# Another table of queue places for the planned order of a conformer block's forward and backward pass

## The chip, the cores and the metric

The program runs on one core of a Trainium2 chip. A core has five engines that run side by side, each with an instruction queue of its own that is taken in order: PE (matrix products and transposes), DVE (vector operations), ACT (activation functions, casts and scaled copies), POOL (general vector work) and SP, which here only starts transfers. PEld in a profile is PE loading its stationary operand. Engines wait for each other by semaphores. The metric is the device time of one execution in microseconds (us).

## The reference

x and grad_out are (2, 4000, 144) in bf16; the kernel returns the output y, the gradient of x and the gradients of seven weights.

```python
xa = layernorm(x)
q, k, v = split(xa @ w_qkv, 3)
p = softmax(q @ k.T * D ** -0.5)               # 4000 x 4000 for each batch
glob = (p @ v) @ w_att_out
u, g = split(gelu(xa @ w_mlp_in), 2)
gc = depthwise_conv(layernorm(g), dw_csgu)     # 5 taps along time
loc = (u * gc) @ w_mlp_out
m = concat(glob, loc)
y = x + (m + depthwise_conv(m, dw_merge)) @ w_merge
# and the gradients of x and of all weights for grad_out
```

## The kernel before

Time is cut into tiles of 125 rows, 32 for each batch. One tile is one step of the attention, forward and backward in one pass. The scores of 125 rows against 4000 columns are made in four chunks of 1000 columns (`ps`, L1580 and L1587). DVE takes the row minimum of the negated scores of each chunk while it copies them to `Pbuf` (L1602) and joins the four (`nm`, L1604); ACT makes the exponentials (L1608). The second set of products in `ps`, the gradient of the probabilities, is cast by ACT to `Sbuf` (L1618) and multiplied with the probabilities by DVE (L1620). Transposing transfers on SP's queue turn `Pbuf` into `PT` (L1612) and `Sbuf` into `ST` (L1794). PE then makes the products with the transposed tiles, `yz` from `PT` (L1629) and `yz` from `ST` (L1667), and the products `X` of both untransposed tiles (L1714), which are added up in `acc` by ACT (L1718) and DVE (L1720). `qt` is the transposed query side of a later tile (L1572), `zt` what is made of `yz`'s result (L1679).

The local branch (gelu, its layer norm, the convolution and their gradients, lines 534 to 710, names that begin with `l_`) is cut into units that run beside the attention steps. Before the attention there is an opening (the class that loads and folds the weights, L119 to L300): ACT and SP start the loads of the raw weights into `raw` (L148, L149, L152); PE transposes some of them (L165, L166); ACT copies them to `two` (L167, L168), which begins with the load of its function table; products of the folded weights follow (L199), then columns and scaled weights (`cols` L212, `sWm` L233). Beside it x is loaded and normalised: DVE's statistics (L358), the normalised rows `xa_aug` (ACT L379, DVE L381, POOL L383), PE's transposes of them (`pt`, L388 and L392), and their copies (ACT L389, DVE L393). `warm` (L187) are matmuls without a use, which keep PE busy in the opening. Near the middle the second batch is prepared in the same way (loads L42, L43; statistics L451 to L458). After the last step, the merge loads `go_h` and `Yg` in blocks of 252 KB (L42, L43), adds up `Hps` on PE (L2000), makes y (L2098 to L2101) and the gradient of x (L2110 to L2127), and a last part makes the weight gradients.

The program is written in one order, and a planner then gives every queue its final order. The class `Planner` gathers the instructions into groups (one instruction each; for PE up to sixteen matmuls), numbers them in written order, and lays them out with a list scheduler over guessed durations. `LEAD` shifts the due time of kinds of groups. At the end of `plan` the table `MOVED` is applied: for each engine it names queue places and the group that shall stand there; all other groups keep their order and fill the places left.

```python
for e in E:
    m = self.MOVED[e]
    put = set(m.values())
    rest = iter([g for g in order[e] if g not in put])
    order[e] = [m[q] if q in m else next(rest) for q in range(len(order[e]))]
```

After that each instruction is tied to the one ahead of it on its engine, so that the queue holds exactly this order. A place in `MOVED` moves one group to it, and shifts all that stand between the old place and the new one by one.

Transfers started by SP and ACT use eight completion semaphores in turn, so an issue also waits until the transfer issued eight before it has landed.

Of the kernel before, what the change touches and what calls it, by code (L numbers as in the profile page):

```python
# [744 lines left out]
class Planner:  # L745
# [98 lines left out]
        "PE": {6: 10, 12: 15, 25: 19, 29: 21, 37: 25, 39: 26, 43: 27, 51: 334, 53: 342, 56: 28, 64: 33, 71: 37, 73: 38, 77: 329, 87: 42, 92: 43, 95: 44,  # L844
            99: 45, 104: 422, 106: 425, 113: 465, 114: 470, 122: 543, 141: 610, 143: 627, 145: 625, 159: 667, 160: 719, 170: 786, 173: 780, 181: 824,
            187: 820, 191: 870, 197: 873, 199: 923, 202: 930, 205: 958, 206: 959, 212: 972, 215: 973, 216: 1000, 220: 1022, 225: 1056, 227: 1075,
            232: 1096, 236: 1104, 246: 1169, 255: 1230, 256: 1222, 260: 1248, 283: 1362, 285: 1373, 288: 1396, 297: 1422, 298: 1431, 305: 1479, 307: 1492,
            308: 1473, 310: 1511, 324: 1570, 328: 1589, 339: 1663, 341: 1651, 342: 1652, 350: 1714, 352: 1723, 357: 1744, 360: 1765, 363: 1768, 382: 1879,
            383: 1910, 399: 1961, 406: 2011, 416: 2064, 419: 2067, 423: 2098, 437: 2149, 445: 2196, 451: 2210, 453: 2261, 455: 2263, 458: 2249, 463: 2311,
            474: 2356, 482: 2407, 492: 2449, 493: 2480, 495: 2467, 502: 2511, 503: 2508, 513: 2561, 516: 2574, 517: 2605, 522: 2606, 523: 2630, 530: 2647,  # L850
            531: 2649, 536: 2702, 540: 2708, 551: 2732, 553: 2787, 556: 2845, 561: 2828, 562: 2831, 564: 2921, 574: 2962, 577: 2957, 584: 2983, 587: 3028,
            605: 3064, 607: 3065, 621: 3173, 625: 3198, 629: 3188, 637: 3247, 638: 3248, 644: 3265, 645: 3283, 651: 3299, 658: 3327, 660: 3328, 675: 3386,
            677: 3387, 678: 3419, 684: 3427, 691: 3453, 694: 3489, 700: 3519, 705: 3552, 710: 3520, 715: 3557, 717: 3598, 719: 3622, 723: 3620, 739: 3696,
            744: 3741, 747: 3766, 757: 3798, 759: 3796, 762: 3818, 769: 3862, 779: 3904, 782: 3930, 786: 3949, 790: 3988, 813: 4084, 822: 4126, 824: 4127,
            826: 4145, 840: 4216, 842: 4235, 846: 4242, 851: 4278, 854: 4290, 858: 4317, 860: 4330, 869: 4368, 874: 4389, 883: 4425, 885: 4463, 888: 4464,
            894: 4498, 895: 4503, 899: 4518, 902: 4548, 911: 4570, 913: 4596, 915: 4607, 918: 4610, 920: 4638, 924: 4655, 940: 4718, 942: 4721, 944: 4749,
            953: 4780, 961: 4843, 963: 4850, 971: 4893, 974: 4915, 977: 4900, 978: 4925, 985: 4987, 990: 4990, 992: 4974, 1001: 5027, 1008: 5078,
            1019: 5134, 1028: 5178, 1032: 5174, 1034: 5195, 1037: 5230, 1041: 5218, 1046: 5274, 1050: 5311, 1054: 5312, 1067: 5362, 1075: 5408, 1086: 5448,
            1089: 5494, 1093: 5508, 1102: 5540, 1105: 5555, 1111: 5612, 1112: 5599, 1117: 5642, 1127: 5667, 1129: 5671, 1132: 5701, 1138: 5726, 1140: 5738,
            1148: 5786, 1156: 5811, 1161: 5881, 1163: 5882, 1175: 5947, 1176: 5919, 1180: 5982, 1182: 5992, 1203: 6075, 1206: 6076, 1208: 6119, 1214: 6128,  # L860
            1219: 6144, 1222: 6186, 1223: 6168, 1227: 6199, 1232: 6206, 1233: 6225, 1237: 6242, 1245: 6266, 1247: 6270, 1251: 6271, 1255: 6292, 1266: 6329,
            1268: 6331, 1273: 6318, 1281: 6335, 1282: 6393, 1283: 6394, 1287: 6402, 1288: 6403, 1289: 6418, 1291: 6419, 1301: 6491, 1302: 6500, 1305: 6516,
            1307: 6525, 1313: 6541, 1318: 6519, 1322: 6528, 1323: 6543, 1324: 6544, 1330: 6607, 1334: 6621, 1338: 6958, 1339: 6635, 1340: 6638, 1342: 6639,
            1346: 6960, 1353: 6671, 1358: 6961, 1360: 6714, 1361: 6715, 1364: 6723, 1365: 6680, 1373: 6850, 1376: 6900, 1380: 6832, 1384: 6875, 1390: 6920,
            1392: 6923, 1394: 6932, 1400: 6980, 1403: 6953, 1404: 6941, 1405: 6950, 1408: 6995, 1409: 6997, 1412: 7000, 1415: 6982, 1418: 7008, 1419: 6983,
            1420: 7056, 1421: 7011, 1424: 7009, 1425: 7012, 1429: 7071, 1430: 7049, 1434: 7108, 1435: 7110, 1438: 7148, 1440: 7151, 1442: 7043, 1443: 7115,
            1444: 7152, 1446: 7084, 1451: 7159, 1453: 7130, 1457: 7160, 1459: 7102, 1462: 7128, 1464: 7175},
        "DVE": {0: 68, 3: 8, 5: 94, 8: 95, 9: 93, 12: 109, 14: 99, 15: 106, 20: 105, 21: 104, 22: 101, 24: 102, 26: 114, 28: 149, 29: 147, 31: 148,
            33: 151, 34: 153, 37: 98, 43: 137, 44: 133, 48: 131, 49: 189, 50: 187, 51: 192, 53: 190, 54: 113, 56: 186, 58: 172, 61: 180, 63: 155, 64: 196,
            65: 195, 69: 174, 70: 213, 72: 219, 74: 194, 77: 217, 78: 235, 79: 233, 84: 268, 100: 396, 110: 419, 111: 466, 116: 490, 117: 491, 120: 492,  # L870
            122: 485, 123: 476, 126: 477, 127: 468, 128: 507, 130: 537, 132: 472, 133: 517, 141: 563, 146: 564, 149: 556, 150: 575, 155: 560, 158: 601,
            165: 618, 167: 636, 171: 640, 172: 695, 174: 648, 176: 641, 180: 661, 181: 697, 182: 664, 184: 698, 188: 686, 190: 744, 193: 743, 196: 709,
            199: 745, 202: 746, 203: 671, 204: 700, 207: 737, 208: 747, 209: 733, 211: 749, 215: 748, 219: 688, 220: 755, 222: 826, 223: 751, 224: 827,
            226: 742, 231: 793, 238: 794, 241: 828, 243: 829, 247: 811, 248: 889, 250: 825, 251: 836, 255: 821, 256: 831, 258: 890, 259: 839, 261: 901,
            264: 842, 265: 844, 266: 843, 269: 845, 270: 861, 271: 846, 272: 862, 275: 882, 276: 880, 279: 886, 280: 914, 283: 898, 286: 916, 287: 909,
            288: 924, 291: 994, 292: 993, 294: 910, 295: 933, 297: 911, 298: 918, 300: 912, 302: 995, 304: 996, 308: 997, 311: 1041, 313: 1042, 315: 1043,
            316: 998, 318: 982, 319: 1044, 323: 1023, 324: 1027, 334: 1046, 337: 1060, 338: 1050, 339: 1053, 341: 1047, 343: 1038, 346: 1055, 348: 1058,
            350: 1092, 356: 1085, 357: 1094, 358: 1135, 361: 1136, 362: 1095, 367: 1113, 371: 1124, 373: 1190, 375: 1142, 378: 1189, 379: 1139, 380: 1159,
            383: 1144, 384: 1170, 386: 1156, 387: 1161, 389: 1149, 391: 1178, 397: 1215, 401: 1180, 402: 1205, 403: 1198, 405: 1217, 408: 1231, 409: 1223,
            412: 1208, 413: 1211, 415: 1236, 416: 1249, 418: 1250, 433: 1343, 434: 1229, 435: 1344, 437: 1303, 438: 1345, 440: 1346, 446: 1348, 447: 1308,  # L880
            453: 1347, 455: 1326, 459: 1351, 463: 1363, 466: 1364, 467: 1393, 469: 1365, 470: 1394, 471: 1389, 477: 1395, 481: 1411, 483: 1400, 484: 1437,
            485: 1401, 486: 1417, 491: 1439, 493: 1440, 495: 1486, 498: 1460, 504: 1462, 506: 1497, 509: 1455, 510: 1448, 512: 1498, 515: 1441, 516: 1499,
            522: 1505, 524: 1482, 527: 1510, 530: 1534, 531: 1533, 533: 1514, 537: 1568, 545: 1552, 550: 1538, 552: 1508, 557: 1680, 558: 1605, 561: 1608,
            565: 1682, 570: 1631, 571: 1624, 577: 1688, 579: 1686, 580: 1628, 581: 1687, 582: 1636, 584: 1645, 585: 1641, 587: 1653, 589: 1650, 592: 1698,
            593: 1655, 595: 1701, 596: 1691, 597: 1699, 598: 1664, 602: 1675, 605: 1715, 606: 1700, 607: 1719, 609: 1724, 612: 1729, 614: 1726, 616: 1745,
            617: 1748, 618: 1734, 627: 1797, 629: 1781, 632: 1783, 634: 1834, 636: 1784, 638: 1810, 644: 1785, 649: 1814, 651: 1794, 654: 1837, 656: 1829,
            657: 1844, 661: 1917, 663: 1861, 665: 1847, 668: 1919, 670: 1920, 672: 1921, 673: 1825, 676: 1980, 678: 1981, 681: 1939, 683: 1912, 691: 1986,
            693: 1927, 694: 1989, 697: 1988, 703: 1999, 704: 1946, 705: 1948, 706: 1934, 707: 1953, 709: 1992, 710: 1962, 712: 1943, 717: 1977, 718: 1965,
# [1671 lines left out]
```

## Time and profile before

| | |
|---|---|
| median of 3 runs | 1230.99 us (1229.53 to 1231.92) |
| the profiled execution | 1230.49 us, its span 1228.7 us |
| mean granted clock of PE | 0.998 |
| PE, DVE, ACT, POOL busy | 1173.0, 1092.6, 937.3, 252.2 us |
| transfers | 196.28 MB, 160 GB/s in the mean |
| transposing transfers `PT`, `ST`, `qt`, `zt` | 126, 126, 62, 62 |

All times in the profile are counted from the start of the span. A row of a timeline has the start, the duration, the engine, the line and the operation, and in brackets how long the engine stood idle ahead of it and what ended that. A row of the chain of waits has a start, a duration and what the end of the program hung on in that time; for a transfer (DMA) it runs from its issue to its landing. A matmul's duration overlaps with that of the next one, since they are pipelined.

### The profile page before, as it was taken

How to read it: one execution, taken by the hardware profiler on the slowest of the kernel's cores; microseconds unless marked ns; L12 is line 12 of the kernel's file. 1: busy time of each engine (PE TensorE's matmuls, PEld its weight loads, DVE VectorE, ACT ScalarE, POOL GpSimd, SP SyncE). 2: the span in 40 equal slices, each digit the busy share in tenths (PEclk: the TensorE clock that was granted, in tenths of full speed). 3: DMA queues.
4: the chain of work that ended last, by engine and by line, in shares of the span. 5: the costliest groups of instructions: out<-in, count | busy, mean ns of one | idle time of the engine just before them, and what ended most of it. 6: DMA issues, size and time to landing. Idle time of an engine off the chain costs nothing.

```text
span 1228.7 us, 36356 instructions
## 1 busy us (share of the span) xinstructions
PE 1173.0 (95%) x14352; PEld 948.9 (77%) x14352; DVE 1092.6 (89%) x3204; ACT 937.3 (76%) x1705; POOL 252.2 (21%) x413
## 2 busy tenths in 40 slices
PE   6999999999999998999999999999999999999998
PEld 4677877777777776777777777778777777899997
DVE  7579999999999998987789999999999998869725
ACT  5899788788897966767988888898888866736541
POOL 7011212111021223210110211101121222124530
PEclk9999999999999999999999999999999999999999
DMA  4578888988697898978987788887888789977653
GB/s 133 130 131 172 162 153 156 166 165 174 130 176 147 157 180 168 197 135 188 177 168 149 145 179 155 162 149 159 166 156 162 151 152 200 177 195 189 168 131 82
DMA packets 672638, 196.28 MB, mean 160 GB/s; under 512 B 647411, under 2 KB 666885, under 8 KB 672445
## 3 DMA queue, kind: packets, MB, share of 16 engines
q1 hardware_dynamic: 671336, 192.56, 79.5%
q8 instruction: 112, 1.84, 0.6%
q0 software_dynamic: 592, 1.18, 0.3%
q14 instruction: 60, 0.49, 0.1%
q10 hardware_dynamic: 538, 0.21, 0.1%
HBM read 23.14 MB, written 16.69 MB: 32 GB/s over the span
## 4 chain that ended last, share of the span: by engine, by line
PE 47%; DVE 26%; DMA 12%; ACT 9%; issue 4%; SPq 1%; POOL 1%; ACTq 0%; DVEq 0%; POOLq 0%
PE X L1714 12%; PE ps L1580 9%; DVE Pbuf L1602 7%; PE yz L1667 6%; PE yz L1629 5%; PE ps L1587 4%; DMA PT<-Pbuf 4%; DVE acc L1720 4%; DVE Sbuf L1620 3%; DMA ST<-Sbuf 2%; ACT Pbuf L1608 2%; DVE l_prod L637 2%; PE po L2098 2%; DMA qt<-qb 2%; PE Hps L2000 2%
## 5 line engine op out<-in xcount | busy, mean ns | idle before, releaser
L1602 DVE TENSOR_SCALAR_CACHE_REDUCE Pbuf<-ps 125x1000 bf16<-125x1000 f32 x256 | 306.2, 1197 | 31.0 <-PE ps L1587 29.8
L1618 ACT CAST Sbuf<-ps 125x1000 bf16<-125x1000 f32 x252 | 251.9, 1000 | 84.1 <-PE ps L1587 81.6
L1608 ACT ACTIVATE Pbuf<-Pbuf,nm 125x1000 bf16<-125x1000 bf16 x256 | 285.5, 1139 | 29.7 <-DVE nm L1604 29.1
L1714 PE MATMUL X<-QBs,Sbuf 125*125 125x144 bf16 x2048 | 298.8, 229 | 2.5 <-DVE acc L1720 0.7
L1714 PE MATMUL X<-QBs,Pbuf 125*125 125x144 bf16 x2048 | 293.9, 226 | 0.4 <-POOL QBs L1651 0.3
L1714 PEld LDWEIGHTS <-Sbuf 125*125 125x125 bf16 x2048 | 260.3, 137 | 28.0 <-issue 26.9
L1580 PE MATMUL ps<-xaT_m,qt 128*125 128x500 bf16 x1024 | 262.7, 375 | 14.6 <-DVE Pbuf L1602 8.2
L1714 PEld LDWEIGHTS <-Pbuf 125*125 125x125 bf16 x2048 | 261.1, 137 | 4.3 <-issue 3.2
L1720 DVE TENSOR_TENSOR acc<-X,acc 125x432 f32<-125x432 f32 (+1 forms) x373 | 201.7, 550 | 11.6 <-PE X L1714 11.3
L1620 DVE TENSOR_TENSOR Sbuf<-Sbuf,Pbuf 125x1024 bf16<-125x1024 bf16 x252 | 172.2, 688 | 1.0 <-ACT Pbuf L1608 0.6
L1580 PEld LDWEIGHTS <-qt 128*125 128x125 bf16 x1024 | 123.9, 137 | 59.9 <-issue 14.6
L1667 PE MATMUL yz<-xa_aug,ST 125*125 125x144 bf16 x2048 | 150.9, 229 | 8.8 <-DMA ST<-Sbuf 6.3
L1629 PE MATMUL yz<-xa_aug,PT 125*125 125x145 bf16 x2048 | 149.4, 228 | 7.4 <-DMA PT<-Pbuf 6.9
L1667 PEld LDWEIGHTS <-ST 125*125 125x125 bf16 x2048 | 139.9, 138 | 17.0 <-issue 8.5
L1629 PEld LDWEIGHTS <-PT 125*125 125x125 bf16 x2048 | 137.5, 137 | 17.3 <-DMA PT<-Pbuf 9.8
L1587 PEld LDWEIGHTS <-qt 16*125 16x125 bf16 x1024 | 36.2, 128 | 98.7 <-issue 98.7
L1651 POOL TENSOR_TENSOR QBs<-g,g 125x144 bf16<-125x144 f32 x64 | 32.8, 513 | 384.0 <-ACT g L1650 229.5
L1587 PE MATMUL ps<-XR,qt 16*125 16x500 bf16 x1016 | 110.9, 420 | 0.0
L593 POOL TENSOR_TENSOR rsr<-ve,mhalf 125x2 f32<-125x2 f32 x32 | 25.7, 803 | 202.9 <-DVE ve L592 152.7
L637 DVE TENSOR_TENSOR l_prod<-ring,Wc 125x720 bf16<-125x720 bf16 x128 | 66.7, 535 | 0.1
L665 POOL TENSOR_SCALAR l_w<-ring,nc,c 125x144 f32<-125x144 bf16 x60 | 30.5, 515 | 138.6 <-DVE nc L661 90.7
L682 POOL TENSOR_TENSOR A_dwc<-l_fl,A_dwc 128x512 f32<-128x512 f32 (+2 forms) x48 | 36.5, 760 | 78.2 <-ACT l_fl L681 77.3
(547 smaller groups left out, 2057.7 us busy)
## 6 DMA issues: line engine op xcount, KB each, us to landing
Yn_d<-yn SPq DMA_DIRECT2D x64, 35.2 KB
Zn_d<-zn SPq DMA_DIRECT2D x64, 35.2 KB
ug_d<-ugr SPq DMA_DIRECT2D x32, 70.3 KB
PT<-Pbuf SPq DMA_TRANSPOSE x126
ST<-Sbuf SPq DMA_TRANSPOSE x126
go_h<-in_grad_out_dram SPq DMA_DIRECT2D x8, 252.0 KB
Yg<-ug_d SPq DMA_DIRECT2D x8, 252.0 KB
Yg<-Yn_d SPq DMA_DIRECT2D x8, 252.0 KB
```

Source lines behind the costliest of these rows:

```text
L637: nc.vector.tensor_tensor(prod[:, bi].rearrange("p a b -> p (a b)"), ring[:, a, p + bi:p + bi + 5, :].rearrange("p a b -> p (a b)"), W.Wc[ ...
L682: nc.gpsimd.tensor_tensor(acc, fl[r0:r1, 0:n], acc, op=ALU.add)
L1580: mm = nc.tensor.matmul(pp[r // 2][:, r % 2, 0:CH], QT[i][:, 2 * h, 0:PB], bs(i)[0].xaT_m[:, c * CH:(c + 1) * CH], start=True, stop=False)
L1587: nc.tensor.matmul(pp[r // 2][:, r % 2, 0:CH], QT[i][rs, 2 * h + 1, 0:PB], xr, start=False, stop=True)
L1602: nc.vector.tensor_scalar(pv(Pbuf, i % NPB, c2), src, -1.0, 3.0e38, op0=ALU.mult, op1=ALU.min, accum_out=NM[i][:, c2:c2 + 1])
L1608: nc.scalar.activation(v, v, ACT.Exp, bias=NM[i][:, 4:5], scale=-1.0)
L1618: nc.scalar.copy(pv(Sbuf, i % NDB, c2), src)
L1620: nc.vector.tensor_tensor(sc, sc, pchunk(i % NPB, c2), op=ALU.mult)
L1629: nc.tensor.matmul(Y, PT[0:PB, j, 0:PB], S.xa_aug[:, j, 0:D + 1], start=(j == 0), stop=(j == NB - 1))
L1667: nc.tensor.matmul(Z, ST[0:PB, j, 0:PB], S.xa_aug[:, j, 0:D], start=(j == 0), stop=(j == NB - 1))
L1714: nc.tensor.matmul(X[:, jj, :], l, r, start=(n_ == 0), stop=(n_ == len(ops) - 1))
L1720: nc.vector.tensor_tensor(av, X[:, 0:nj, :], av, op=ALU.add)
```

## The change

Only the literal table `MOVED` is exchanged. `LEAD`, the scheduler, the guessed durations and all that builds the program stay, so both programs hold the same 14352 matmuls, 2662 vector operations, 1712 activations and copies, 413 POOL operations and 931 transfers on SP's queue; only the order on the five queues differs. The table is 22 lines longer, so what stood on line 1580 stands on 1602 afterwards, and so on.

| engine | entries before | entries after | the same in both | group moved in both, to another place or the same |
|---|---|---|---|---|
| PE | 302 | 330 | 87 | 177 |
| DVE | 1123 | 1272 | 95 | 762 |
| Activation | 576 | 629 | 76 | 325 |
| Pool | 139 | 164 | 24 | 86 |
| SP | 475 | 507 | 26 | 327 |

The first entries of each engine, and those of SP in the last attention steps and the merge (places 716 to 745):

```diff
     MOVED = {
-        "PE": {6: 10, 12: 15, 25: 19, 29: 21, 37: 25, 39: 26, 43: 27, 51: 334, 53: 342, 56: 28, 64: 33, 71: 37, 73: 38, 77: 329, 87: 42, 92: 43, 95: 44,
+        "PE": {11: 163, 16: 167, 24: 19, 26: 20, 29: 21, 31: 22, 35: 25, 37: 26, 44: 27, 51: 334, 53: 28, 54: 342, 55: 29, 61: 31, 64: 33, 71: 37, 79: 38,
...
-        "DVE": {0: 68, 3: 8, 5: 94, 8: 95, 9: 93, 12: 109, 14: 99, 15: 106, 20: 105, 21: 104, 22: 101, 24: 102, 26: 114, 28: 149, 29: 147, 31: 148,
+        "DVE": {0: 68, 1: 9, 5: 94, 6: 95, 11: 91, 12: 106, 14: 111, 16: 99, 17: 104, 18: 110, 19: 101, 21: 102, 23: 107, 24: 105, 25: 148, 26: 98,
...
-        "Activation": {0: 55, 4: 57, 5: 58, 6: 56, 8: 123, 12: 244, 14: 252, 15: 245, 17: 126, 18: 134, 19: 249, 20: 247, 24: 128, 26: 253, 28: 177,
+        "Activation": {2: 58, 7: 57, 11: 126, 12: 59, 13: 247, 16: 141, 20: 128, 21: 250, 23: 248, 24: 56, 26: 253, 28: 249, 31: 60, 35: 216, 37: 212,
...
-        "Pool": {0: 86, 1: 70, 2: 71, 6: 83, 7: 85, 8: 87, 9: 52, 12: 49, 13: 51, 14: 48, 18: 136, 27: 214, 30: 387, 32: 221, 33: 264, 36: 144, 37: 181,
+        "Pool": {0: 86, 1: 70, 2: 47, 3: 49, 4: 51, 5: 71, 7: 84, 8: 50, 10: 82, 11: 52, 12: 87, 15: 103, 17: 136, 18: 132, 20: 142, 27: 236, 28: 260,
...
-        "SP": {5: 62, 7: 64, 9: 7, 11: 67, 12: 73, 13: 77, 15: 88, 18: 76, 19: 63, 20: 391, 22: 256, 23: 261, 24: 165, 25: 259, 26: 257, 27: 166, 28: 65,
+        "SP": {4: 5, 5: 62, 7: 7, 8: 78, 11: 6, 12: 75, 15: 88, 17: 72, 19: 81, 20: 256, 21: 165, 22: 77, 23: 261, 24: 391, 27: 355, 28: 73, 29: 258,
...
-            709: 6259, 710: 6092, 712: 6191, 715: 6125, 717: 6146, 718: 6174, 719: 6277, 721: 6194, 722: 6058, 723: 6158, 724: 6192, 725: 6258, 726: 6246,
-            727: 6222, 728: 6132, 730: 6213, 731: 6195, 732: 6214, 733: 6257, 735: 6221, 738: 6159, 740: 6273, 741: 6236, 742: 6280, 745: 6157, 751: 6372,
+            716: 6196, 717: 6106, 718: 6065, 720: 6146, 721: 6127, 722: 6246, 724: 6193, 725: 6221, 726: 6222, 727: 6281, 729: 6277, 730: 6258, 731: 6194,
+            734: 6236, 735: 6255, 737: 6259, 738: 6058, 739: 6157, 741: 6257, 742: 6213, 743: 6132, 744: 6298, 745: 6256, 750: 6388, 751: 6385, 752: 6372,
```

What it does at the places that matter below, in the names of the kernel:

- In the opening ACT starts three transfers (the two of w_qkv and dw_merge) ahead of its table load; the four of w_mlp_out and w_att_out stand behind, between its copies and scaled weights. Two of the `sWm` (L233) stand behind the `xa_aug` (L379) they stood ahead of. DVE's first minimum (L1602) stands ahead of the copy of the third block of transposes (L393). Of the warm-up matmuls, five stand ahead of the first L392 and four behind it, where there were one and five.
- At the batch change SP starts the loads of x (`xa_aug`) ahead of those of grad_out (`gq`).
- In the step near 600 us the sixteen matmuls of L1667 of one half of a tile stand some 8 us of PE's work later, next to those of the other half, and the scores stand ahead of the products `X` that they followed.
- In the last attention step the loads `go_h` and `Yg` of 252 KB that stood ahead of the transposing transfer `ST` in SP's queue stand behind it, and so do the other large ones of that stretch. PE's first `Hps` (L2000) stand behind the last product `X` of one more tile part, some 8 us of PE's work later.
- In all steady steps, single vector operations, activations, transfers and matmul groups change places with their neighbours.

422 rows, old and new, of the table MOVED are left out of this document.

## The prediction

> **What bounds the kernel now.** I read the page's busy times and its chain first, then the busy time of each engine by stage, then the timelines at the places where an engine that bounds a stage stands idle.
>
> ```profile
> PE 1173.0 (95%) x14352; PEld 948.9 (77%) x14352; DVE 1092.6 (89%) x3204; ACT 937.3 (76%) x1705; POOL 252.2 (21%) x413
> PE 47%; DVE 26%; DMA 12%; ACT 9%; issue 4%; SPq 1%; POOL 1%; ACTq 0%; DVEq 0%; POOLq 0%
> ```
>
> The whole program leaves PE idle for 1228.7 - 1173.0 = 55.7 us, DVE for 136.1. The shares are means over unlike stages, so the table by stage decides (columns: stretch, its length, then busy time and count of PE, PEld, DVE, ACT, POOL, the granted clock, the DMA share, GB/s):
>
> ```profile
> 30.00:97.00 67.00, 63.69 (x675) 46.28 (x674) 45.31 (x108) 63.59 (x133) 8.30 (x14) 1.00 0.62 126
> 100.00:450.00 350.00, 338.56 (x4035) 268.68 (x4032) 344.76 (x1010) 291.79 (x522) 62.49 (x94) 1.00 0.86 162
> 520.00:600.00 80.00, 78.70 (x957) 62.60 (x955) 66.93 (x154) 61.69 (x108) 9.13 (x19) 1.00 0.83 166
> 600.00:640.00 40.00, 35.44 (x400) 28.11 (x399) 29.60 (x79) 36.66 (x71) 3.49 (x5) 0.96 0.92 175
> 640.00:1000.00 360.00, 352.07 (x4216) 279.82 (x4214) 353.37 (x1019) 299.94 (x534) 60.78 (x94) 1.00 0.83 158
> 1050.00:1224.00 174.00, 171.37 (x2571) 160.99 (x2570) 116.24 (x419) 84.23 (x164) 52.05 (x80) 1.00 0.68 160
> ```
>
> ACT is close to the bound from 30 to 97 us, DVE from 100 to 450 (5.2 us idle) and from 640 to 1000 (6.6 us idle), PE from 520 to 600 and from 1050 to the end (2.6 us idle in 174). An order of the same instructions can only take idle time from the engine that bounds its stage. So the places to look at are the opening, the seams near 478 and 601 us, and the few waits of PE in the last stage.
>
> **The change, part by part.** Only the table of places is changed: the same matmuls, vector operations, activations and transfers, in another order on every queue. Nothing is removed or added, so every term is a wait that goes, shrinks or appears. I laid the new order beside the old one and looked up, at each stall of the old trace, where the waiting instruction and what it waits for now stand. The sum is made against the profiled execution, 1230.49 us: its span of 1228.7 and 1.8 around it.
>
> *The opening.* ACT now issues three transfers ahead of its table load where it issued seven. The four that go behind are these (start, duration), with what follows them on ACT:
>
> ```profile
> 4.57 0.44 ACTq L148 DMA_DIRECT2D raw<-in_w_mlp_out_dram  x1
> 5.17 0.38 ACTq L149 DMA_DIRECT2D raw<-in_w_mlp_out_dram  x1
> 6.19 0.34 ACTq L149 DMA_DIRECT2D raw<-in_w_att_out_dram  x1
> 7.28 0.39 ACTq L148 DMA_DIRECT2D raw<-in_w_att_out_dram  x1
> 7.71 1.28 ACT L167 ACT_TABLE_LOAD   x1 [7.71 <-DMA raw<-in_w_att_out_dram]
> 9.00 0.46 ACT L167 COPY two<-hps 128x144 bf16<-128x144 bf16 x2
> 12.80 0.71 ACT L233 ACTIVATE sWm<-raw,cols 128x144 bf16<-128x144 bf16 x2
> ...
> 29.90 1.13 ACT L1608 ACTIVATE Pbuf<-Pbuf,nm 125x1000 bf16<-125x1000 bf16 x1
> ```
>
> and this is what PE does meanwhile (in brackets the idle time ahead of it and who ended it):
>
> ```profile
> 7.97 0.18 PE L166 MATMUL hps<-ident,raw 16*16 16x16 bf16 x1
> 9.51 0.84 PE L199 MATMUL hps<-two 128*128 128x144 bf16 x4 [1.37 <-ACT two L167]
> 13.96 1.02 PE L388 MATMUL pt<-ident,xa_aug 125*128 125x125 bf16 x8 [3.18 <-ACT xa_aug L379]
> 15.83 1.27 PE L187 MATMUL warm<-wz 128*128 128x256 bf16 x5
> ```
>
> Four fewer issues are 0.44 + 0.38 + 0.34 + 0.39 = 1.55 us, so the table load can end 1.5 us or more earlier, at 7.4, and the copies are then held by PE's transposes, the last of which ends at 8.15. L199 should start 0.7 to 1.1 us earlier. On ACT the pair of L233 at 12.80 (0.71) now stands behind the last xa_aug that PE's L388 waits for, and one issue (0.44) ahead of it: 0.3 more. L388 thus starts 1.0 to 1.4 earlier, I take 1.2. Against it: of the warm-up matmuls (five in 1.27 us, 0.25 each), nine now stand between L388 and the first projection, where there were six: three more, about +0.7. The four issues, 1.55 us, now lie among ACT's copies; what hides them is ACT's waiting ahead of 29.90. If that cover is gone, they cost up to 1.55, since ACT bounds what follows.
>
> ```profile
> 22.76 0.69 DVE L393 COPY R<-pt 16x1000 bf16<-16x1000 bf16 x1 [1.42 <-PE pt L392]
> 23.48 1.20 DVE L1602 TENSOR_SCALAR_CACHE_REDUCE Pbuf<-ps 125x1000 bf16<-125x1000 f32 x1
> 29.71 0.16 DVE L1604 TENSOR_REDUCE nm<-nm 125x1 f32<-125x4 f32 x1
> ```
>
> DVE waited 1.42 us for transposes although the scores of the first L1602 were ready; now L1602 stands ahead of that copy. It brings up to 1.42, and nothing where PE's later scores set nm (29.71); I take 0.5. The opening: -1.2 + 0.7 - 0.5 = -1.0, with the ends +0.7 (the warm-up alone counts) and -2.6 (all of 1.2 and 1.42).
>
> *The batch change.* The loads of x for the second batch move ahead of the loads of grad_out in SP's queue. The chain of waits and DVE's timeline show
>
> ```profile
> 478.27 5.17 DMA xa_aug<-in_x_dram
> 483.54 0.73 DVE L451 BATCH_NORM_STATS2 pst<-xa_aug 125x6 f32<-125x144 bf16 x3 [0.59 <-DMA xa_aug<-in_x_dram]
> ```
>
> The transfer is 5.17 us long, but DVE stood still for 0.59 of it only. Gain 0 to 0.6, I take 0.2.
>
> *The seam at 601 us.* Here everything stood still behind one transposing transfer:
>
> ```profile
> 596.22 5.41 DMA ST<-Sbuf
> 601.67 1.77 PE L1667 MATMUL yz<-xa_aug,ST 125*125 125x144 bf16 x16 [1.55 <-DMA ST<-Sbuf]
> 602.77 0.46 DVE L577 TENSOR_TENSOR l_z<-l_a,l_hs 125x576 bf16<-125x576 bf16 x1 [2.29 <-ACT l_a L574]
> 606.53 1.20 DVE L1602 TENSOR_SCALAR_CACHE_REDUCE Pbuf<-ps 125x1000 bf16<-125x1000 f32 x1 [2.06 <-PE ps L1587]
> 604.92 0.52 ACT L1718 COPY acc<-X 125x432 f32<-125x432 f32 x1 [0.21 <-PE X L1714]
> 607.43 0.52 ACT L1718 COPY acc<-X 125x432 f32<-125x432 f32 x1 [1.32 <-PE X L1714]
> ```
>
> PE waits 1.55 us in front of that L1667, with the products X and the next scores queued behind it; ACT and DVE then wait for those. In the new order these sixteen matmuls stand some 8 us later, next to their other half, and the scores ahead of the products. ACT carries this stage (36.66 of 40), so the gain is at most its two waits, 0.21 + 1.32 = 1.53. I take 1.0: what L1667 feeds comes later, and something of the wait can come back there. Ends 0 and -1.5.
>
> *The last attention step.* SP issues two loads of 252 KB each just ahead of a transposing transfer:
>
> ```profile
> 1066.52 0.34 SPq L42 DMA_DIRECT2D go_h<-in_grad_out_dram  x1
> 1069.37 0.58 SPq L42 DMA_DIRECT2D Yg<-ug_d  x1
> 1070.12 8.26 DMA ST<-Sbuf
> 1078.42 1.23 PE L1667 MATMUL yz<-xa_aug,ST 125*125 125x144 bf16 x16 [1.79 <-DMA ST<-Sbuf]
> 1070.00:1080.00 10.00, 8.21 (x119) 7.31 (x117) 5.91 (x11) 4.41 (x7) 1.64 (x3) 1.00 0.98 197
> ```
>
> It lands after 8.26 us, where the one above took 5.41, and PE, which bounds the stage, waits 1.79 us: all that PE lacks in these 10 us (8.21 busy). In the new order both loads, and the other large ones of this stretch, stand behind that transfer. 2.85 us less of landing would cover the 1.79. I take -1.5, since small loads still stand ahead; ends 0 and -1.8. What is late next are the loads themselves: they feed L2000, which the new order puts behind some 8 us more of PE's products, about as far as the loads move.
> The Trainium skill ("DMA: Bandwidth & Descriptors", section "Queues, rings and completion order") says that each transfer engine takes one issuer's descriptors in the order of the ring. By that alone the 504 KB ahead, at the 197 GB/s of the row, would be 2.6 us of the 8.26 (an estimate), this term -1.8 and the sum -4.0.
>
> *Everything else.* The steady stages have hundreds of entries of their own. Waits that the old trace shows there are often answered by a producer that stands 0.6 to 2 us earlier; what other instructions now wait for, the old trace cannot show. The gain cannot exceed DVE's idle 5.2 + 6.6 us; a loss is bounded by nothing but the waits that exist. I take 0, with 3 us to either side: a quarter of that idle time.
>
> The sum is -1.0 - 0.2 - 1.0 - 1.5 = -3.7: 1230.49 - 3.7 = 1226.8. The median of the three runs, 1230.99, lies 0.5 above the profiled one, so 1227.3; I say 1227.2.
>
> **The rivals.**
>
> *No change that can be measured, about 1230.* The gains lie at seams; the stages behind are bound by another engine. For it: of 67 us from 30 on, ACT is busy 63.59, and now has four issues (1.55) to place before it, so the opening can come to +0.7; DVE's late data at 601 can return as a wait for the moved L1667 (its 1.55). Then only the -1.5 at 1078 is left, with half a microsecond of losses: 1230.99 - 1.0 = 1230. Against it: the two PE and ACT waits are on the engine that bounds the stage.
>
> *Slower, about 1235: transposing transfers come late.* PE's waits for transfers were
>
> ```profile
> PE yz L1629 <- DMA PT<-Pbuf: 6.9, 12, 0.9
> PE yz L1667 <- DMA ST<-Sbuf: 6.3, 5, 1.8
> PE ps L1580 <- DMA qt<-qb: 4.8, 6, 1.2
> ```
>
> 18.0 us in 23 waits, 0.78 each, over 64 tiles. SP's queue is taken in order; its table changes most of its places, and every load or store that moves ahead of a transpose delays it, as at 1070. Against the sum of -3.7, 0.2% slower (2.5) needs 6.2 us, eight more such waits on the path. Ten give 7.8: 1227.3 + 7.8 = 1235. For it: DVE leaves so little idle that one late tile is not made up. Against it: the worst two of these waits, 1.79 and 1.55, are the ones that the order undoes.
> The Trainium skill's rule on the same page ("Rules for kernel authors") is to issue a transfer early and wait late; the loads that the change moves behind would by it be exposed in turn. No row here shows it yet.
>
> *Much faster, about 1222.* The ends add up: -2.6 - 0.6 - 1.5 - 1.8 = -6.5, and -3 from the steady stages: 1221.5. For it speak the many earlier producers; against it, that all ends must come together.
>
> **How the numbers follow.** The forecast has 0.48 (its own range 1224.5 to 1228.4), much faster 0.07, no change 0.19, slower 0.26. What a measurement of this kernel can tell from no change is about 0.2%, 2.5 us: faster 0.55, same 0.19, slower 0.26. The range goes from 1221.5, the sum of the ends, up to 1234.5, near the slower case, with about 0.07 left below and 0.12 above.
>
> **What would show it.** In the changed profile: the table load starting near 5 to 6 us and L388 near 12.8; the first exponential (29.90) near 29; no wait of DVE for x near 483; no wait over 1 us at L1667 near 600, and DVE not idle for over 2 us there; ST near 1070 landing in 6 us or less and PE over 9.5 busy in the ten microseconds after. DVE's idle time from 100 to 450 and 640 to 1000 should stay near 12 us, PE's waits for PT, ST and qt near 18 less 3.3. I am wrong if these waits grow by 6 us, or if DVE's idle time in the steady stages moves by more than 3.

## The result, and the profile after

| | before | after |
|---|---|---|
| median | 1231.45 us (1229.53 to 1232.70, 4 runs) | 1216.04 us (1212.67 to 1222.33, 4 runs) |
| the profiled execution | 1230.49 us, span 1228.7 | 1215.52 us, span 1213.7 |
| mean granted clock of PE | 0.998 | 0.999 |

The ratio is 0.9882, with an interval of 0.984 to 0.9925: 1.2% faster, 15.4 us by the medians. A second set of runs, told below, gave 0.9907 (0.9873 to 0.9941). The direction was predicted, the time was not: 1227.2 was said, and the range ended at 1221.5. Lines of the kernel after are 22 higher (1580 is 1602 now), those of the experiments' kernels 45 higher.

The busy times and the shares of the chain:

```profile
PE 1168.9 (96%) x14352; PEld 947.3 (78%) x14352; DVE 1085.6 (89%) x3204; ACT 936.3 (77%) x1705; POOL 254.7 (21%) x413
PE 55%; DVE 20%; ACT 12%; DMA 8%; issue 3%; SPq 2%; POOL 1%; ACTq 0%; DVEq 0%; POOLq 0%
```

The chain hangs on transfers for 8% of the span where it was 12%. DVE's idle time fell by 8.0 us (136.1 to 1213.7 - 1085.6 = 128.1), and its busy time by 7.0, though it runs the same instructions. The second number is the one that the prediction had ruled out.

The table by stage of the kernel after, in the columns of the prediction:

```profile
30.00:97.00 67.00, 63.35 (x678) 46.57 (x677) 46.67 (x114) 64.42 (x136) 8.88 (x17) 1.00 0.66 133
100.00:450.00 350.00, 342.80 (x4092) 272.08 (x4091) 348.16 (x1028) 293.94 (x528) 64.81 (x98) 1.00 0.85 166
520.00:600.00 80.00, 77.01 (x929) 61.24 (x929) 64.48 (x149) 67.56 (x120) 7.35 (x13) 1.00 0.87 175
600.00:640.00 40.00, 37.62 (x457) 30.25 (x455) 36.62 (x108) 34.96 (x65) 3.74 (x7) 1.00 0.81 163
640.00:1000.00 360.00, 353.82 (x4231) 281.77 (x4230) 353.17 (x1026) 298.67 (x532) 67.20 (x96) 1.00 0.82 161
```

A stretch of fixed times holds other work after an order has changed, so its idle time is compared with care. DVE's idle time from 100 to 450 went from 5.2 to 1.8 us and from 640 to 1000 from 6.6 to 6.8; ACT's from 30 to 97 went from 3.4 to 2.6.

The longest sums of PE's waits (in total, times, longest):

```profile
PE ps L1602 <- DVE Pbuf L1624: 7.2, 14, 0.9
...
PE yz L1651 <- DMA PT<-Pbuf: 3.9, 5, 1.9
...
PE ps L1602 <- DMA qt<-qb: 1.6, 1, 1.6
...
PE pm L1945 <- POOL Yr L2007: 1.4, 1, 1.4
...
PE yz L1689 <- DMA ST<-Sbuf: 0.9, 2, 0.4
```

Waits of PE for `PT`, `ST` and `qt` are 3.9 + 1.6 + 0.9 = 6.4 us in 8, where they were 18.0 in 23; the longest one for `ST` is now 0.4.

To see where the 15 us lie, the trace is cut where DVE joins the minima of a tile (`nm`), which every tile does once. This is worked out from the two traces, in us:

```
tiles            start  0-4   4-10  10-16  16-25  25-34  34-37  37-45  45-59  59-63   end
before            29.7  69.7  96.6   99.1  149.8  147.8   56.3  125.1  231.1   60.0  163.5
after             28.7  68.3  96.9   96.0  147.0  144.4   53.9  128.5  224.3   61.9  163.8
difference        -1.0  -1.4  +0.3   -3.1   -2.8   -3.4   -2.4   +3.4   -6.8   +1.9   +0.3
```

There is no one place: five stretches gain 2 to 7 us each, two lose 2 to 3. These are two single executions; what is chance in them shows only beside the traces of the experiments.

### The profile page after: what moved, and what is told of

Its sections match the earlier page's. It is cut to its first block, busy times and chain, and to the rows that moved or that the text cites. A ratio compares the mean times of both kernels' runs of the same rounds, so it can differ in the third digit from the quotient of the medians.

```text
span 1213.7 us, 36291 instructions
## 1 busy us (share of the span) xinstructions
PE 1168.9 (96%) x14352; PEld 947.3 (78%) x14352; DVE 1085.6 (89%) x3204; ACT 936.3 (77%) x1705; POOL 254.7 (21%) x413
## 4 chain that ended last, share of the span: by engine, by line
PE 55%; DVE 20%; ACT 12%; DMA 8%; issue 3%; SPq 2%; POOL 1%; ACTq 0%; DVEq 0%; POOLq 0%
PE X L1736 15%; PE ps L1602 10%; PE yz L1651 7%; PE yz L1689 7%; DVE Pbuf L1624 5%; PE ps L1609 4%; DVE acc L1742 3%; DMA PT<-Pbuf 3%; ACT Sbuf L1640 3%; DVE Sbuf L1642 3%; ACT Pbuf L1630 3%; PE po L2120 2%; PE Hps L2022 2%; DVE l_prod L637 1%; DMA ST<-Sbuf 1%
## 5 line engine op out<-in xcount | busy, mean ns | idle before, releaser
L1630 ACT ACTIVATE Pbuf<-Pbuf,nm 125x1000 bf16<-125x1000 bf16 x256 | 287.4, 1142 | 29.5 <-DVE nm L1626 28.8
L1602 PE MATMUL ps<-xaT_m,qt 128*125 128x500 bf16 x1024 | 261.2, 375 | 10.6 <-DVE Pbuf L1624 7.2
L1602 PEld LDWEIGHTS <-qt 128*125 128x125 bf16 x1024 | 123.6, 137 | 54.0 <-issue 12.2
L1673 POOL TENSOR_TENSOR QBs<-g,g 125x144 bf16<-125x144 f32 x64 | 33.9, 529 | 415.2 <-ACT g L1672 312.2
L665 POOL TENSOR_SCALAR l_w<-ring,nc,c 125x144 f32<-125x144 bf16 x60 | 32.7, 550 | 135.5 <-DVE nc L661 60.0
L2147 ACT ACTIVATE t<-t,dx_c,rstd_x 125x144 f32<-125x144 f32 x64 | 28.8, 500 | 32.5 <-DVE t L2146 32.4
```

Source lines behind the costliest of these rows:

```text
L1602: mm = nc.tensor.matmul(pp[r // 2][:, r % 2, 0:CH], QT[i][:, 2 * h, 0:PB], bs(i)[0].xaT_m[:, c * CH:(c + 1) * CH], start=True, stop=False)
L1630: nc.scalar.activation(v, v, ACT.Exp, bias=NM[i][:, 4:5], scale=-1.0)
L1673: nc.gpsimd.tensor_tensor(QBs[:, i % NPB, 1, :], g0[:], g1[:], op=ALU.add)
```

## The experiments

Each kernel has a table that names every place of every queue. `old[e]` and `new[e]` are the orders of queue `e` in the kernels before and after, `t[g]` is the start of group `g` in the trace of before. Cuts were put where both orders have done nearly the same work. Ratios are to the kernel before on the same chip, with a 95% interval; times are medians, and a gain in us is the ratio's distance from 1, of 1232 us.

### How far into the program the gain is made

```diff
-    order[e] = old[e]
+    order[e] = [g for g in new[e] if t[g] < END] + [g for g in old[e] if t[g] >= END]
```

with END at 99, 445, 640 and 1000 us.

> The changed order on all five queues for the work that started in the first 99 us of the old trace, the old order for everything after. Theory spread (the gain is made a little at a time in every stage, most of it in the steady ones, where I had put 0): 2 to 3 us faster than before, as the two traces differ at the fifth tile (99.37 against 96.98). Rival seams (the gain sits at a few places of the opening, the batch change, 601 and the last step, each worth more than I thought): 4 us or more faster here. Rival tail of the execution (the two traces differ by chance and the curve of progress cannot be read): anything else.

> The changed order up to 445 us of the old trace (the steady stage of the first batch with it), the old one after. Spread: 8 us faster than before (444.96 against 436.87 at the 26th tile), so 5 to 6 more than with the opening alone. Seams: no more than the opening alone gives, 2 to 4 us.

> The changed order up to 640 us of the old trace, the old one after. Spread: 13 to 14 us faster than before (649.07 against 635.16), the batch change and the stage of ACT up to 640 giving 5 to 6 of them. Seams: 4 to 6 us in all.

> The changed order up to 1000 us of the old trace, the old one in the last steps, the merge and the end. Spread: 16 to 17 us faster than before, which is 1 to 2 us faster than the whole change, since from the 60th tile to the end the changed trace lost 2. If the term of the last step was right after all, this kernel is 1 to 2 us slower than the whole change.

| changed up to | ratio | median, us |
|---|---|---|
| nothing | 1 | 1233.08 (18 runs) |
| 99 us | 0.9951 (0.9934 to 0.9968) | 1227.23 |
| 445 us | 0.9934 (0.9909 to 0.9960) | 1225.93 |
| 640 us | 0.9876 (0.9852 to 0.9901) | 1218.84 |
| 1000 us | 0.9873 (0.9845 to 0.9901) | 1218.42 |

Two stretches make most of the gain: the first 99 us (-6.0) and 445 to 640 (-7.1). The steady stages add 2.1 and 0.4, which the intervals do not tell from nothing.

### One queue's order at a time

```diff
-    order["SP"] = old["SP"]
+    order["SP"] = new["SP"]
```

The other queues are moved only as far as their dependences then force. `a_dve` does the same with DVE; `b_sp` is the kernel after with SP's queue back in the old order.

> The old order with SP's queue alone in the changed order; on the other queues only what SP's order forces is moved. Theory transfers (the changed order gains because transposing transfers reach PE in time: PE's waits for PT, ST and qt fell from 18.0 us to 5.5 + about 1): most of the gain, 8 us or more faster than before, with PE's waits for transfers under 10 us. Rival vector (DVE's own order makes the gain, by less idle time and fewer operations beside POOL's): under 3 us. Rival fit (only all queues together gain): no faster, or slower than before.

> The old order with DVE's queue alone in the changed order, the others moved only as far as that forces. Transfers: under 3 us faster than before, PE's waits for transfers still 15 us or more. Vector: 8 us or more faster. Fit: no faster, or slower than before.

> The changed order with SP's queue put back into the old order, the others moved only as far as that forces. Transfers: at 1225 us or above, within 5 us of before. Vector: within 4 us of the whole change. Fit: slower than the whole change by 8 us or more, and not faster than before.

They gave 1.1204 (1.1176 to 1.1232), 1.0864 (1.0837 to 1.0890) and 1.2218 (1.2187 to 1.2250): 1382, 1340 and 1507 us. PE's longest waits with SP's queue alone changed

```profile
PE yz L1674 <- DVE zn L1716: 24.7, 13, 5.5
```

and with SP's alone put back

```profile
PE ps L1625 <- DVE Pbuf L1647: 52.7, 47, 9.1
PE yz L1674 <- DVE zn L1716: 48.7, 21, 8.8
```

are for DVE, not for transfers. PE's clock suffers as well: in the three profiles it was granted at half for 120, 41 and 205 us, where the profile of before has 3.4. These kernels are not one queue's order alone, though. To fit SP's new order, 112 instruction groups of PE, 140 of DVE and 77 of ACT had to leave the old one, and those queues then follow neither kernel. So the runs show that an order so mixed loses 9 to 22%; how much of that comes from the one queue and how much from the forced moves is open, and so is whether any single queue "has" the gain.

### The middle alone, and its parts

```diff
-    order[e] = old[e]
+    order[e] = [g for g in old[e] if t[g] < A] + [g for g in new[e] if A <= t[g] < B] + [g for g in old[e] if t[g] >= B]
```

with A and B at 445 and 640; at 459.4 and 570.1 (the batch change); at 570.1 and 624.35 (the seam near 601).

> The changed order only for the work that started between 445 and 640 us of the old trace (batch change, the stage in which PE and then ACT bound), the old order before and after. The kernels with the changed order up to 445 and up to 640 differ by 7 us. If stages add up: 5 to 9 us faster than before. If the gain there hangs on where the stages before it end: under 3 us.

> The changed order only for the work that started between 459.4 and 570.1 us of the old trace, where both orders have done the same work at both ends: the batch change. Prediction: 0.2 us faster, at most 0.6. If stages add up (0.9924 for 445 to 640 less 0.9966 for 570 to 624): 4 to 6 us faster.

> The changed order on all queues only for the work that started between 570.1 and 624.35 us of the old trace, where both orders have done the same work at both ends; the old order elsewhere. Theory clock (a long wait of PE there costs its length and then 3.4 us at half the granted clock, in nearly every run): 4 to 6 us faster than before, the tiles 35 and 36 together 34 us long instead of 36 to 40. Rival, my own step (only the wait of 1.55 us is to be had, ACT's two waits bound it): 1 to 1.5 us faster.

445 to 640 alone gave 0.9924 (0.9902 to 0.9947), the batch change 0.9963 (0.9947 to 0.9978), the seam 0.9966 (0.9949 to 0.9983). In us that is -9, -4.6 and -4.2; the two parts add up to the whole.

At the seam the two stalls of PE are gone. Its rows with the seam alone changed

```profile
612.21 2.19 PE L1712 MATMUL yz<-xa_aug,ST 125*125 125x144 bf16 x32
615.54 2.24 PE L1674 MATMUL yz<-xa_aug,PT 125*125 125x145 bf16 x32
```

have no wait ahead of either. The trace of before has the 1.55 that the prediction showed and a second one behind it:

```profile
616.79 2.24 PE L1629 MATMUL yz<-xa_aug,PT 125*125 125x145 bf16 x32 [0.89 <-DMA PT<-Pbuf]
```

That profile was a mild one. The kernel with the first 99 us changed has the old order here, and shows

```profile
602.28 1.23 PE L1712 MATMUL yz<-xa_aug,ST 125*125 125x144 bf16 x16 [2.92 <-ACT l_a L574]
617.73 3.88 PE L1674 MATMUL yz<-xa_aug,PT 125*125 125x145 bf16 x32 [2.69 <-DMA PT<-Pbuf]
```

2.92 + 2.69 instead of 1.55 + 0.89 (the wait is put down to whichever came last, here ACT). In seven traces with the old order here the first of these stalls lasted 1.0 to 3.5 us. The second lasted 0.9 to 2.8 in five of them, in two put down to `qt`, and two have none. Over the same seven traces, the two tiles of this seam took 36.0 to 39.5 us, 37.8 in the mean, and the 36.0 is the one that was priced. Seven traces with the changed order gave 33.3 to 35.0, 33.9 in the mean. The difference, 3.9, agrees with the 4.2 measured.

At the batch change the wait that the prediction named has stayed, at 0.60 with this stretch alone changed:

```profile
477.83 0.73 DVE L451 BATCH_NORM_STATS2 pst<-xa_aug 125x6 f32<-125x144 bf16 x3 [0.60 <-DMA xa_aug<-in_x_dram]
...
468.52 0.64 DVE L670 SCALAR_TENSOR_TENSOR l_dd<-l_dgn,rsr,l_w 125x144 bf16<-125x144 bf16 x2
```

What went is something else, in the second row. In the trace of before the same operation of DVE stands beside POOL's sums:

```profile
466.85 1.27 POOL L682 TENSOR_TENSOR A_dwc<-l_fl,A_dwc 128x512 f32<-128x512 f32 x1
...
466.81 1.47 DVE L670 SCALAR_TENSOR_TENSOR l_dd<-l_dgn,rsr,l_w 125x144 bf16<-125x144 bf16 x1
...
469.32 0.63 DVE L670 SCALAR_TENSOR_TENSOR l_dd<-l_dgn,rsr,l_w 125x144 bf16<-125x144 bf16 x1
```

It takes 1.47 us instead of 0.36, and ends 0.16 after POOL does (466.81 + 1.47 against 466.85 + 1.27). With the changed order two of them take 0.64 together: 1.4 us of DVE's time are gone, and in all seven traces with the changed order here neither takes more than 0.37. That is 1.4 of the 4.6; where the other 3.2 come from the traces do not settle (tiles 25 to 34 are only 0.7 shorter in this kernel's profile than before's 147.8, and 1.3 shorter than the mean of the other traces with the old order here).

### Which queues the seam needs

```diff
-    order["PE"] = old["PE"]
+    order["PE"] = [g for g in old["PE"] if t[g] < 570.1] + [g for g in new["PE"] if 570.1 <= t[g] < 624.35] + [g for g in old["PE"] if t[g] >= 624.35]
```

for PE alone (30 places), for SP alone (45 places), and for both.

> As the last, but only PE's queue takes the changed order in that stretch (30 places; three on DVE move with it). If the later place of the sixteen matmuls and the earlier scores make the gain, as the prediction had it: as fast as the kernel with all queues changed there, within 2 us. If the order of the queues has to fit together even here: no faster than before, or slower.

> The old order, with only SP's queue in the changed order between 570.1 and 624.35 us of the old trace (45 places; five on PE and three on ACT move with it). Theory transfers (in the old order PT is issued behind the acc_d stores, the ring store and qt, and PE then waits 0.9 to 2.8 us for it near 617 in five of five traces; the changed order issues it earlier): 3 to 5 us faster than before, no wait of PE for PT over 1 us near 617, tile 36 at 14 to 15 us. Rival fit: SP's order alone gives nothing, as PE's alone did, under 1.5 us either way.

> The old order, with PE's and SP's queues in the changed order between 570.1 and 624.35 us of the old trace (30 and 45 places; three each on DVE and ACT move with them). Theory pair (PE's order removes the wait for ST near 604, SP's the wait for PT near 617, and each alone leaves the other): 3 to 5 us faster than before, tiles 35 and 36 together 33 to 35 us, no wait of PE over 1.2 us near 604 or 617. Rival fit (ACT's and DVE's orders are needed too): under 1.5 us.

PE alone gave 0.9993 (0.9977 to 1.0009), SP alone 1.0008 (0.9988 to 1.0027), both 0.9980 (0.9965 to 0.9996), where all five queues gave 0.9966. With PE alone the wait for `ST` is gone, but

```profile
620.89 2.24 PE L1674 MATMUL yz<-xa_aug,PT 125*125 125x145 bf16 x32 [2.50 <-DMA PT<-Pbuf]
```

the wait for `PT` is as long as ever. With SP alone it is the wait for `ST` that stands:

```profile
609.64 1.63 PE L1712 MATMUL yz<-xa_aug,ST 125*125 125x144 bf16 x16 [2.69 <-DMA ST<-Sbuf]
```

and none for `PT` is there. That SP's order removed it is not shown: four of the seven traces with the old order have no wait over 0.4 for `PT` here either, and this profile is of the longest of the kernel's twelve runs (1242.62 us, the median is 1233.52). With both, neither is left:

```profile
601.29 2.24 PE L1674 MATMUL yz<-xa_aug,PT 125*125 125x145 bf16 x32 [0.17 <-DMA PT<-Pbuf]
...
617.83 2.19 PE L1712 MATMUL yz<-xa_aug,ST 125*125 125x144 bf16 x32
```

By the medians about half of the gain is missing, though the intervals of 0.9980 and 0.9966 overlap. The traces show a reason: the two tiles ahead of the seam take 31.4 us with PE's order, with and without SP's, where they take 29.7 in the old order and 29.5 with all five queues changed. In both traces PE stands 1.2 us for DVE's `acc` there. So the moves on the other three queues seem to belong to it; none of them was tried alone.

### The opening, split

The same edit with the ends at 0 and 33 us, and at 33 and 101 us.

> The changed order only for the first 32.95 us of the old trace. Prediction: 1.0 us faster. If the opening carries what the first 99 us gave (0.995): 4 to 7 us faster. If the rest of those 99 us, in which ACT bounds, carries it: 1 to 2 us faster. The first tile's minimum at 28.7 to 29.1 us in the trace instead of 29.7 to 30.6.

> The changed order only for the work that started between 32.95 and 100.95 us of the old trace, where ACT bounds. If it carries what the first 99 us gave beyond the first 33: 3 to 6 us faster than before. If the lengths of tiles in the traces tell it (68.3 against 69.7 for tiles 0 to 4): 1 to 2 us.

The opening gave 0.9986 (0.9971 to 1.0001), -1.7 us; 33 to 101 gave 0.9977 (0.9959 to 0.9995), -2.8 us. Together that is 4.5 against the 6.0 of the first 99 us; the intervals, each some 2 us to either side, cover the difference. In the second stretch the window from 30 to 97 us of this kernel

```profile
30.00:97.00 67.00, 63.95 (x690) 47.12 (x689) 46.22 (x113) 64.41 (x135) 8.48 (x15) 1.00 0.67 132
```

has ACT, which is nearest to the bound there, busy 64.41 us instead of 63.59, with two activations more: 0.8 us less idle, as in the kernel after. Tiles 0 to 4 take 68.1 to 68.6 us in all traces with the changed order there and 69.7 in those with the old order; the interval does not tell this from 2.8.

### The end alone

A at 1014.15, B at the end.

> The old order up to 1014 us, the changed order from there to the end: the term of the last attention step alone, with the merge and the end. Prediction: 1.5 us faster. Theory accident (the wait of 1.79 us at 1078 stood in two of six traces that have the old order there, so its removal is worth little, and the loads that are late now cost PE later): 2 to 4 us slower than before.

1.0011 (1.0001 to 1.0021): 1.4 us lost, where the prediction had a gain of 1.5. The wait at `ST` is gone, here and in the kernel after, where PE is 9.69 busy in the ten microseconds that answer to those of the prediction:

```profile
1060.00:1070.00 10.00, 9.69 (x155) 9.53 (x154) 5.88 (x13) 4.78 (x9) 1.51 (x3) 1.00 0.76 201
```

But that wait, 1.79 us in the profile of before, was a matter of chance: of twelve traces with the old order there, seven have it (1.54 to 2.86 us) and five do not. And the changed order has a new one ahead of it. In this kernel's trace PE waits

```profile
1019.53 1.17 PE L1674 MATMUL yz<-xa_aug,PT 125*125 125x145 bf16 x16 [1.13 <-DVE zn L1716]
```

for `zn`, which DVE makes of `yz`'s result; in the twelve traces such waits in the last four tiles are under 0.4. These tiles take 62.2 us here and 61.9 and 62.4 in two profiles of the kernel after, where the twelve have 59.5 to 61.1. Which of the moves makes them longer is open.

The kernel after has one more new wait, in the merge, of POOL and then of PE:

```profile
1143.04 0.66 POOL L2007 COPY Yr<-Yg 125x576 bf16<-125x576 bf16 x1 [3.38 <-DMA Yg<-Yn_d]
...
1147.13 0.63 PE L1945 MATMUL pm<-ident,Yr 125*80 125x125 bf16 x8 [1.40 <-POOL Yr L2007]
```

It stands in both of its profiles (1.40 and 1.44 us), but not in the one with the end alone changed. So it is no part of the 1.4 us lost there, and that the load it waits for is one of those moved behind `ST` is not shown.

### The best of both, and the whole again

Changed order up to 669.2 us and from 766.9 to 1014.15, old order elsewhere; and the changed kernel a second time.

> The changed order up to 669.2 us and from 766.9 to 1014.15 us of the old trace, the old order in the two stretches where its tiles were shorter in every trace that has it (tiles 40 to 45 by 3.4 us, from tile 60 on by 3.8). If the lengths of stages add up: 1209 us, 5 to 7 us below the whole change. If a stage's length hangs on the one ahead: within 2 us of the whole change.

> The whole change again, timed beside the others. 0.986 to 0.991 of before; the sum of the stages run alone (to 99, 445 to 640, 1014 to the end, and what the kernels up to 445 and up to 1000 add) is 15 us, or 0.988.

The mixture gave 0.9892 (0.9864 to 0.9919), 1220.76 us; the whole change 0.9907 (0.9873 to 0.9941), 1220.29 us (1214.65 to 1229.88). Leaving out the two losing stretches should have given some 5 us more, and nothing can be told. Either these stretches cost less than single traces say, or cutting there costs as much; that stays open. No version is shown to beat the kernel after.

## Why the prediction was wrong

Stage by stage, in us; the measured ones are from the ratios of the kernels above, with some 2 us to either side, and 4 where two kernels are subtracted (from 101 to 445 and from 640 to 1000).

| step | predicted | measured |
|---|---|---|
| the opening | -1.0 (+0.7 to -2.6) | -1.7 |
| the batch change | -0.2 (0 to -0.6) | -4.6 |
| the seam at 601 | -1.0 (0 to -1.5) | -4.2 |
| the last attention step, with the end | -1.5 (0 to -1.8) | +1.4 |
| everything else | 0 (3 to either side) | -2.8 from 33 to 101, about -2 to 445, -0.4 from 640 to 1000 |
| sum | -3.7 | -14 by the parts, -15.4 and -12.5 by the medians of the whole |

*The opening* came out near its sum. The rows of the kernel after that answer to it are

```profile
4.96 1.28 ACT L167 ACT_TABLE_LOAD   x1 [4.96 <-DMA raw<-in_w_qkv_dram]
7.84 0.68 PE L199 MATMUL hps<-two 128*128 128x144 bf16 x4 [0.37 <-ACT two L167]
12.38 1.09 PE L388 MATMUL pt<-ident,xa_aug 125*128 125x125 bf16 x8 [3.44 <-ACT xa_aug L379]
28.70 0.16 DVE L1626 TENSOR_REDUCE nm<-nm 125x1 f32<-125x4 f32 x1
28.96 1.14 ACT L1630 ACTIVATE Pbuf<-Pbuf,nm 125x1000 bf16<-125x1000 bf16 x1
```

The table load starts 2.75 us earlier, L199 1.67 (0.7 to 1.1 was said), L388 1.58 (1.0 to 1.4), the first `nm` 1.01: 29.71 to 28.70, the -1.0 of the sum. The first exponential comes at 28.96, "near 29". L199 and L388 thus came earlier than their ranges, and what followed gave that back, so the exact -1.0 is in part luck.

*The steps that failed* are the caps of the batch change ("Gain 0 to 0.6") and of the seam ("the gain is at most its two waits, 0.21 + 1.32 = 1.53"). Both rest on one sentence: "An order of the same instructions can only take idle time from the engine that bounds its stage." The runs showed two things against it.

First, idle time in one execution is one draw, and a stall of PE costs more than its length. The seam's stall, 1.55 us in the profile of before, was up to 3.5 in other executions of the same order, and the second stall, 0.89 in the profile and 2.2 to 2.8 in four others, was not priced at all. PE is either busy or waiting in these two tiles, so their length can be split. In the mean of seven traces each, the waits fell from 5.2 to 3.4 us, and PE's busy time from 32.7 to 30.5 for nearly the same matmuls (352 and 354). The second part is the clock. In six of the seven traces with the old order it is granted at half for 3.4 or 6.8 us inside these tiles, each time from the end of one of these stalls or shortly before or behind it, and in none with the changed order; half of that time is 2.2 us in the mean. Together, 1.8 + 2.2, this is the 3.9 by which the tiles became shorter. ACT's idle time in one profile held neither part.

Second, busy time depends on the order as well. The groups of DVE's L670 before and after (busy, mean ns of one):

```profile
L670 DVE SCALAR_TENSOR_TENSOR l_dd<-l_dgn,rsr,l_w 125x144 bf16<-125x144 bf16 x64 | 25.1, 412 | 0.2 <-POOL l_w L665 0.2
```

```profile
L670 DVE SCALAR_TENSOR_TENSOR l_dd<-l_dgn,rsr,l_w 125x144 bf16<-125x144 bf16 x64 | 22.4, 363 | 0.2 <-POOL l_w L665 0.2
```

are the same 64 operations, 412 - 363 = 49 ns shorter each, 3.1 us in all. Take every operation of DVE that lasts over 0.2 us longer than the median of its group (same line, operation and shape, more than eight of them). There were 36 in before, 19.6 us of excess, and 28 after, 15.1 us, and each of them in both traces runs beside an instruction of POOL. From 100 to 1000 us, where DVE is closest to its bound, the excess is 9.0 us in before, 6.9 to 8.0 in eight more traces with the old order in all or nearly all of it, and 4.8 and 5.3 in the two traces of the whole change. Some 3 us of DVE's time there are thus not idle time, and the prediction's bound on the gain did not hold them. That they went into the end time one for one is argued, not shown: no run changed only the neighbours on POOL.

*The last attention step* had the right mechanism for the one wait it priced and left out the rest. That wait is worth some 1.3 us in the mean of the twelve traces, not 1.79. "What is late next are the loads themselves ... about as far as the loads move" was taken as nothing, and the new order of the last four tiles was not looked at. They became some 2 us longer, with 1.13 for `zn`; in the kernel after 1.40 for `Yr` come on top, not at L2000 (the consumer that was named) but at a transpose fed through POOL. The end alone came to +1.4; how that divides is open.

*Everything else* was taken as 0. The stage that ACT carries, 33 to 101 us, was left out and gave 2.8. The steady stages measured 2.1 and 0.4, inside the 3, but these small sums hide larger parts. Tiles 10 to 25 are 5.5 us shorter in the mean of six traces with the changed order than in eleven with the old one, and the two sets do not overlap. The kernel with the change up to 445 us may show only 2.1 of this because its next tiles, 25 to 34, are long (151.1 us, 147.8 to 149.1 in five traces with the old order). DVE's idle time in these stages went from 11.8 to 8.6 us, by 3.2, where the prediction had named more than 3 as a sign of being wrong. Its other signs, as far as the trace shows them, came as said, but for the wait of DVE for x, which is still 0.56 in the kernel after, and PE's waits for transfers, 6.4 where 14.7 was said. In the steady stages the waits for `ST` of the kind

```profile
235.26 1.23 PE L1667 MATMUL yz<-xa_aug,ST 125*125 125x144 bf16 x16 [1.20 <-DMA ST<-Sbuf]
```

are gone after, and the tile that held this one takes 12.2 us instead of 14.6. But tiles 37 to 45 lose 3.4 again: 127.6 to 128.5 us in three traces with the changed order, 124.2 to 125.7 with the old one. The transfer of `PT` there is late, on the chain of the kernel after and on PE's timeline:

```profile
677.37 6.64 DMA PT<-Pbuf
684.05 1.23 PE L1651 MATMUL yz<-xa_aug,PT 125*125 125x145 bf16 x16 [1.86 <-DMA PT<-Pbuf]
```

*The rivals.* "Much faster" (1222) had the sign and not the size, since it added up the same caps. "Slower, transposing transfers come late" is refuted in the sum, 18.0 us of these waits to 6.4, and true at one place, 684 us. "No change" had the opening at up to +0.7, with the four issues of ACT still to place; the opening gained, and what the issues cost in it does not show.

## What to carry to other kernels

Price a stall from several executions of the same program: one profile gave 1.55 us where others gave 1.0 to 3.5, and a cap made from it was too low by a factor of nearly three. Look behind the stall, too: here half of what it cost was matmuls at half the clock. An order can also shorten busy time, by taking a vector operation out from beside another engine's; look at the longest single operations of a line, not only at idle time. And try an order by stretches of time with all queues together: exchanging one queue, with what that forces on the others, cost 9 to 22%.

## What the runs showed of the hardware

*PE's clock drops behind short waits.* After the 1.55 us wait at 601.7 the windows of before show

```profile
603.00:604.00 1.00, 1.00 (x11) 1.00 (x10) 0.44 (x2) 1.00 (x3) 0.00 (x0) 0.50 0.30 75
604.00:605.00 1.00, 1.00 (x9) 0.91 (x8) 0.48 (x1) 0.79 (x4) 0.00 (x0) 0.50 0.24 47
```

a granted clock of 0.50 (the first number behind the brackets), and those of after the same behind the 1.86 at 684:

```profile
686.00:687.00 1.00, 1.00 (x11) 1.00 (x10) 1.00 (x5) 0.43 (x2) 0.00 (x0) 0.50 0.59 133
```

A drop lasts 3.4 us, sometimes twice that. In 17 traces, behind the first 100 us, 46 waits of PE lasted 1.5 us or more; 20 drops came with them or shortly behind, none without such a wait, and not every wait brought one (in the trace with the first 99 us changed, the 2.92 ahead of 602.28 did not, the 2.69 ahead of 617.73 did). The Trainium skill ("TensorE: Matmul & The Clock Gate", "Why this matters for your kernels") warns of idle gaps of PE over about 3 us, but here half of that gap sufficed. The length of the drop agrees with the window of about 3.4 us that the same page gives under "What's actually happening". Of the whole gain the drops are a small part: the mean granted clock over all runs went from 0.9973 to 0.9988 with the whole change, which is 1.8 us of PE's time. At the seam they are a larger one: 0.9971 to 0.9983 with it alone changed, 1.5 us of 4.2, and 2.2 by the traces above. A better clock alone does not shorten the program: with PE's part of the seam alone it was 0.9992 and nothing was gained that can be told; PE waited 8.2 us in the two tiles there.

*The opening at half rate, by chance.* With the changed order up to 445 us, the profiled execution had

```profile
23.36 0.42 PE L187 MATMUL warm<-wz 128*128 128x256 bf16 x1
```

0.42 us for a matmul that took 0.27 at 20.85 with the change up to 640 us, with the same instructions in the opening. The first record of the full clock in that trace is at 28.0 us, in the nineteen other traces at 15.4 to 19.9, although PE had no wait over 0.15 us there from 17.0 on. Its first `nm` came at 33.4 us instead of 28.9. This may be why runs of the changed order spread over 10 to 15 us; one profile shows it, so that is open.

*A vector operation held by POOL.* L670 beside L682 took 1.47 us instead of 0.36 and ended just behind it; at this place of the old order it took 1.468 to 1.475 us in each of ten traces. The Trainium skill ("SBUF — State Buffer", section "SBUF: two separate sides") says that a pair of ports is shared by DVE and POOL under an exclusive lock: a DVE operation with two SBUF inputs and a POOL operation that reads SBUF do not run together, and the later one is blocked until the other has ended. L670 has two such inputs, L682 adds in SBUF, and the trace agrees in that L670 ended 0.16 behind L682. Which came first it does not settle: by the records L670 started 0.04 ahead (466.81 against 466.85), while POOL's operation before L682 was still running.
